# Holding the routing to one step behind each turned block, with the second expert's gathers issued in a row

## The chip, the cores and the metric

One core of one Trainium2 chip runs the whole program in one launch. The metric is the device time of one execution in microseconds (us); a kernel is timed in several runs and stands for the median. The engines are TensorE (PE, with its weight loads PEld), VectorE (DVE), ScalarE (ACT), GpSimd (POOL) and SyncE (SP, which issues most DMAs). Each works through its own queue in order and waits for the others by semaphores.

## The reference

Attention with a sigmoid in place of a softmax gives 3584 rows of 768 numbers. A greedy router gives each row to one of 8 experts, 448 rows each, and the expert applies two matrix products with a ReLU between.

```python
scores = scale * np.matmul(q, k.transpose(0, 1, 3, 2)) - np.log(S)      # 8 x 12 heads, S = 448, head_dim 64
attn = 1.0 / (1.0 + np.exp(-scores)); x = attn @ v                      # as [3584, 768]
logits = x @ w_gate                                                     # [3584, 8]
# all (token, expert) pairs from the highest logit down: a token takes an expert
# if the token is free and the expert has fewer than 448 tokens
for e in range(8):
    h = np.maximum(x[assigned == e] @ w1[e], 0.0)                       # [448, 768] @ [768, 1024]
    out[assigned == e] = h @ w2[e]                                      # [448, 1024] @ [1024, 768]
```

## The kernel before, in words

The first 300 us are attention; they are not touched. The router then fills one expert after another, in the order in which experts become full: phase 0 ahead of the first expert, phases 1 to 7 beside the experts' products.

An expert is 320 matmuls of the generator `moe` (356 for the first, which cuts its first tile in two): 144 for the first layer (lines 673, 675, 677: rows `xh`, `xl` against weights `wh`, `wl`, three products for one, since each fp32 number is split in a high and a low part), then 176 for the second layer (line 715) in two halves of four units of 22. A weight unit is loaded by SP three units ahead and split two units ahead: `wh` on ACT (line 598), `wl` on POOL (line 600).

Between two experts stands the next expert's input. `gather` (line 620, POOL) fetches four blocks of rows (128, 128, 128 and 64) into `xr` by the list `r_idx`. `xturn` (lines 634 to 638) turns a block in two halves: three PE transposes into a PSUM tile `tp`, of which there are two, then `xh` on ACT, then `xl` on DVE; `xl` is the last reader, so the next block's transposes wait for it. `scatter` (lines 645 and 646, POOL) writes an expert's result rows, four blocks again.

Routing phases are nearly all DVE work. A phase is a generator: `remove` (lines 302 to 306) and `keys` (lines 147 to 154, ending in `r_KT`), then two PE transposes of `r_KT` (line 163), the copy `r_KE` and 16 search steps (lines 174 to 213: three counts over 224 numbers, then small operations), then `pick`, `place` (line 253 to 264) and `lists` (lines 273 to 294), which leaves `r_idx`.

Nothing is scheduled by a tool. The loop at the end of `moe_attention` draws one matmul at a time from `moe(kx)` and adds its planned cost to a clock of its own (189 ns in the first layer, 164 ns in the second). By that clock it writes a routing step when the one before has had its planned time plus `SLACK` (every 2175 ns for a search step), and at most one item of the list `chores` (gathers, turns, scatters, each with a due time) every 1000 ns. What is still due when an expert ends is written at once by `flush`. So the clock sets only the order of the instructions; the times come from the engines.

Of the kernel before, what the change touches and what calls it, by code (L numbers as in the profile page):

```python
# [28 lines left out]
T_KEYS, T_KE, T_STEP, T_DVE, T_KAP, T_PICK, T_TOT, T_OH, T_BT = 3600, 2100, 2050, 2025, 500, 2600, 600, 3800, 600  # L29
SLACK = 150  # L30
CHORE_NS = 1000
TURN_NS = 2500
H_POOL = 8
EARLY = 1
FIRST = 4000.0
# [300 lines left out]
def moe_attention(tc, q, k, v, w_gate, w1, w2, out):  # L336
# [7 lines left out]
    with contextlib.ExitStack() as ctx:  # L344
# [269 lines left out]
        def blocks():  # L614
            for j in range(4):
                yield j, min(128, S - 128 * j)

        def gather(kx, j, n):
            t = xg[kx, j] = xp.tile([128, DM], F32, name="xr", bufs=XR_BUFS)
            nc.gpsimd.indirect_dma_start(out=t[:n], out_offset=None, in_=xs,  # L620
                                         in_offset=bass.IndirectOffsetOnAxis(ap=listed[kx][:n, j:j + 1], axis=0))

        def xturn(kx, j, n, hf, wide):
            if (j, hf) == (0, 0):
                XH[kx] = (xp.tile([128, ND, S], F32R, name="xh", bufs=2),
                          xp.tile([128, ND, S], F32R, name="xl", bufs=2))
            xh, xl = XH[kx]
            if wide and hf:
                p = ps_s.tile([128, 2, 512], F32, name="sc")[:, 0]
            else:  # L630
                p = ps_t.tile([128, 512], F32, name="tp")
            for i in range(3):
                dd = hf * 3 + i
                nc.tensor.transpose(p[:, i * n:(i + 1) * n], xg[kx, j][:n, dd * 128:(dd + 1) * 128], ident[:n, :n])  # L634
            pv = p[:, :3 * n].rearrange("p (a t) -> p a t", a=3)
            sl = (slice(None), slice(hf * 3, hf * 3 + 3), slice(j * 128, j * 128 + n))
            nc.scalar.activation(xh[sl], pv, AF.Copy)
            nc.vector.tensor_tensor(xl[sl], pv, xh[sl].bitcast(F32), OP.subtract)  # L638

        scat, chores = [], []  # L640
# [105 lines left out]
        for j, n in blocks():  # L746
# [5 lines left out]
            if j == 1:  # L752
                for _ in range(EARLY):
                    next(route)
        t_route, t_chore = FIRST, 1500.0
        for kx in range(E):
            turned = kx + 1 == E
            start = clock[0]

            def prepare():  # L760
                t0 = clock[0]
                lag = max(5000, min(14000, start + 40000 - t0))
                for j, n in blocks():
                    chores.append((t0 + 1500 * j, kx + 1, lambda j=j, n=n: gather(kx + 1, j, n)))
                for j, n in blocks():
                    chores.append((t0 + lag + TURN_NS * j, kx + 1,
                                   lambda j=j, n=n: [xturn(kx + 1, j, n, hf, False) for hf in range(2)]))

            def flush(kx):
                for c in [c for c in chores if c[1] <= kx]:  # L770
                    chores.remove(c)
                    c[2]()

            for step, cost in enumerate(moe(kx)):
                clock[0] += cost
                t = clock[0]
                if kx == 0 and step == 35:
                    flush(0)
                if t >= t_route:
                    t_route = t + next(route, 0) + SLACK  # L780
                if not turned and kx + 1 in listed:
                    prepare()
                    turned = True
                if t >= t_chore:
                    c = next((c for c in chores if c[0] <= t), None)
                    if c:
                        chores.remove(c)
                        c[2]()
                        t_chore = t + CHORE_NS
            if not turned:  # L790
                while kx + 1 not in listed:
                    next(route)
                prepare()
            flush(kx + 1)
# [28 lines left out]
```

## Time and profile before

| | |
|---|---|
| median of 3 runs | 876.28 us (876.18 to 877.7) |
| the profiled execution | 874.18 us, of which 872.4 us are the span of the profile |
| PE busy in the span | 823.4 us (94%), 5523 matmuls |
| DVE busy | 533.9 us (61%) |
| ACT, POOL busy | 437.9 us (50%), 485.5 us (56%) |
| first matmul of experts 0 to 7 | 328.8, 401.8, 469.6, 536.8, 605.3, 671.9, 739.3, 803.7 us |

A row of the timeline has the start in us from the span's start, the duration in us, the engine, the line, the operation with its output and inputs, and in brackets how long the engine had idled before it and who ended that. PE rows overlap: in the second layer a matmul's row is 0.33 to 0.34 us long and the next one starts 0.17 us after it. Experts are numbered from 0 in the order in which they run.

### The profile page before, as it was taken

The numbers are of one execution on the slowest core, as the hardware profiler recorded it, in microseconds if no ns is written. First come the engines' busy times: TensorE is split into PE (matmuls) and PEld (weight loads), VectorE is DVE, ScalarE is ACT, GpSimd is POOL, SyncE is SP. The second block draws the span as 40 slices with busy tenths as digits, with TensorE's granted clock in tenths as the row PEclk, the third lists the DMA queues.
The fourth block names the chain that finished last, engine by engine and source line by source line (L and its number), as shares of the span: only waits on it lengthen the run. The fifth ranks groups of instructions, "written<-read, shape, count | busy, mean of one in ns | idle before, by whom it ended". The sixth has DMA issues, their size and how long they took to land.

```text
span 872.4 us, 16402 instructions
## 1 busy us (share of the span) xinstructions
PE 823.4 (94%) x5523; PEld 650.5 (75%) x5523; DVE 533.9 (61%) x2047; ACT 437.9 (50%) x602; POOL 485.5 (56%) x510
## 2 busy tenths in 40 slices
PE   6999999999998829998999999999999999999996
PEld 3455455455455719998989889898899899899996
DVE  4665555555554978969879889789699620221211
ACT  6777777777775714424424433443434343444431
POOL 9645444444400024866865875865785874853643
PEclk9999999999999958999999999999999999999998
DMA  9876656666612954344354443452553543533421
GB/s 171 172 144 127 132 122 122 129 124 126 131 38 81 323 192 134 107 149 150 110 153 138 112 152 136 113 170 91 154 154 109 162 136 120 190 121 106 147 81 64
DMA packets 195573, 117.60 MB, mean 135 GB/s; under 512 B 144192, under 2 KB 185152, under 8 KB 195488
## 3 DMA queue, kind: packets, MB, share of 16 engines
q1 hardware_dynamic: 182752, 83.03, 36.6%
q0 software_dynamic: 10880, 33.28, 12.2%
q8 instruction: 44, 0.72, 0.4%
q10 hardware_dynamic: 1856, 0.23, 0.2%
q14 instruction: 41, 0.34, 0.1%
HBM read 94.47 MB, written 22.02 MB: 134 GB/s over the span
## 4 chain that ended last, share of the span: by engine, by line
PE 80%; DVE 11%; POOL 3%; issue 2%; DMA 2%; SPq 1%; ACT 0%; ACTq 0%; POOLq 0%; DVEq 0%
PE sc L715 22%; PE tp L463 13%; PE sc L439 11%; PE sc L675 8%; PE sc L673 8%; PE sc L677 8%; DVE r_junk L174 4%; PE tp L469 3%; PE sc L449 2%; PE tp L634 2%; PE tp L484 1%; POOL out_dram L646 1%; POOL xr L620 1%; PE rt L285 1%; POOL wl L600 1%
## 5 line engine op out<-in xcount | busy, mean ns | idle before, releaser
L600 POOL TENSOR_TENSOR wl<-wr,wh 128x768 fp32r<-128x768 f32 x110 | 202.3, 1853 | 32.3 <-ACT wh L598 32.0
L715 PE MATMUL sc<-wh,hb 128*128 128x384 f32 x768 | 200.4, 339 | 0.0
L429 ACT ACTIVATE at<-sc,bias 128x896 f32<-128x896 f32 x168 | 160.9, 1006 | 63.2 <-PE sc L449 38.2
L374 POOL DMA_DIRECT2D nkq<-in_q_dram x188 | 118.3, 645 | 111.6 <-DVE kqT L414 104.8
L677 PE MATMUL sc<-xh,wl 128*128 128x448 f32 (+2 forms) x396 | 144.6, 365 | 1.4 <-POOL wl L600 1.4
L675 PE MATMUL sc<-xl,wh 128*128 128x448 f32 (+2 forms) x396 | 144.9, 366 | 0.0
L673 PE MATMUL sc<-xh,wh 128*128 128x448 f32 (+2 forms) x396 | 144.9, 366 | 0.0
L715 PEld LDWEIGHTS sc<-wh,hb 128*128 128x128 f32 x768 | 138.1, 188 | 1.8 <-issue 0.7
L715 PE MATMUL sc<-wl,hb 128*128 128x384 f32 x384 | 129.5, 337 | 0.3 <-POOL wl L600 0.3
L598 ACT ACTIVATE wh<-wr 128x768 fp32r<-128x768 f32 x128 | 104.1, 851 | 51.0 <-PE sc L715 30.7
L174 DVE TENSOR_SCALAR_CACHE_REDUCE r_junk<-r_KE,r_T 128x224 bf16<-128x224 f32 x315 | 123.3, 441 | 0.1
L463 PE MATMUL tp<-at,nv 128*64 128x448 f32 x576 | 118.6, 547 | 0.0
L683 ACT ACTIVATE hb<-sc 128x768 fp32r<-128x768 f32 x32 | 26.0, 814 | 142.4 <-PE sc L677 142.4
L423 DVE TENSOR_TENSOR kqL<-kqT,kqH 128x896 fp32r<-128x896 f32 (+1 forms) x49 | 52.5, 1072 | 58.3 <-ACT kqH L421 58.2
L689 POOL TENSOR_TENSOR hb<-h,hb 128x768 fp32r<-128x768 f32 x32 | 59.2, 1850 | 49.9 <-ACT h L686 46.7
L620 POOL DMA_INDIRECT xr<-xs,r_idx x32 | 31.5, 984 | 96.5 <-ACT wh L598 79.8
L600 DVE TENSOR_TENSOR wl<-wr,wh 128x768 fp32r<-128x768 f32 x18 | 23.8, 1329 | 96.9 <-ACT wh L598 96.8
L463 PEld LDWEIGHTS tp<-at,nv 128*64 128x64 f32 x576 | 37.1, 136 | 59.4 <-issue 58.0
L677 PEld LDWEIGHTS sc<-xh,wl 128*128 128x128 f32 x396 | 75.0, 189 | 8.2 <-POOL wl L600 1.7
L675 PEld LDWEIGHTS sc<-xl,wh 128*128 128x128 f32 x396 | 75.1, 190 | 7.0 <-DVE xl L638 0.4
L673 PEld LDWEIGHTS sc<-xh,wh 128*128 128x128 f32 x396 | 75.1, 190 | 6.8 <-issue 0.4
L715 PEld LDWEIGHTS sc<-wl,hb 128*128 128x128 f32 x384 | 72.1, 188 | 0.8 <-POOL wl L600 0.6
(163 smaller groups left out, 1257.2 us busy)
## 6 DMA issues: line engine op xcount, KB each, us to landing
wr<-in_moe_w_dram SPq DMA_DIRECT2D x128, 384.0 KB, 3.2
xs<-xr SPq DMA_DIRECT2D x32, 336.0 KB, 4.3
nkq<-in_k_dram SPq DMA_DIRECT2D x190, 56.0 KB, 2.6
nkq<-in_q_dram POOLq DMA_DIRECT2D x188, 56.0 KB, 2.7
nv<-in_v_dram SPq DMA_DIRECT2D x92, 96.0 KB, 2.4
nr<-in_v_dram SPq DMA_DIRECT2D x46, 32.0 KB, 2.3
xr<-xs,r_idx POOLq DMA_INDIRECT x32, 4.6
out_dram<-yr,r_idx POOLq DMA_INDIRECT x32, 3.6
```

Source lines behind the costliest of these rows:

```text
L174: nc.vector.tensor_scalar(junk, KE, T[:, i:i + 1].bitcast(F32), None, OP.is_ge, OP.add, accum_out=cnt[:, i:i + 1])
L374: qn.dma_start(t[o:o + 32, n], rws[x])
L429: nc.scalar.activation(a, p[:, :, :S], AF.Sigmoid, bias=bias, scale=1 / math.sqrt(D))
L439: nc.tensor.matmul(p[:, j, :S], R[half, c * 128:(c + 1) * 128], M[half], start=i == 0, stop=i == 2)
L463: nc.tensor.matmul(p[j * 64:j * 64 + 64, :S], nat["v", b, g][:, h0 + j, c, :], AT[b, pr, c][:, j, :], start=(c == 0), stop=(c == 2 and pr ...
L598: nc.scalar.activation(hi, raw[u], AF.Copy)
L600: eng.tensor_tensor(lo, raw[u], hi.bitcast(F32), OP.subtract)
L673: nc.tensor.matmul(ph[:, f, lo:hi], wh[:, a, fs], xh[:, dd, lo:hi], start=st, stop=False)
L675: nc.tensor.matmul(ph[:, f, lo:hi], wh[:, a, fs], xl[:, dd, lo:hi], start=False, stop=False)
L677: nc.tensor.matmul(ph[:, f, lo:hi], wl[:, a, fs], xh[:, dd, lo:hi], start=False, stop=en)
L689: nc.gpsimd.tensor_tensor(h2, h0[:, :, t], h1.bitcast(F32), OP.subtract)
L715: nc.tensor.matmul(o, hs, w[:, a], start=st and n == 0, stop=en and n == len(terms) - 1)
```

## The change

When the next expert's list is done, `prepare` enters its gathers and turns in `chores`. Three things differ.

- While blocks remain to be turned, from 2500 ns (`HOLD_NS`) before the first is due, a routing step is written only if a block has been turned since the last one: one step behind each block at most. Ahead of the second expert (`kx` = 0) not even that: no routing step until all four blocks are turned.
- Blocks are due every 3200 ns of the planned clock in place of 2500; ahead of the second expert every 1300.
- The second expert's four gathers are written in a row, at once.

```diff
-TURN_NS = 2500
+TURN_NS = 3200
+TURN_FIRST = 1300
+HOLD_NS = 2500
...
             def prepare():
                 t0 = clock[0]
                 lag = max(5000, min(14000, start + 40000 - t0))
-                for j, n in blocks():
-                    chores.append((t0 + 1500 * j, kx + 1, lambda j=j, n=n: gather(kx + 1, j, n)))
-                for j, n in blocks():
-                    chores.append((t0 + lag + TURN_NS * j, kx + 1,
-                                   lambda j=j, n=n: [xturn(kx + 1, j, n, hf, False) for hf in range(2)]))
+                if kx:
+                    for j, n in blocks():
+                        chores.append((t0 + 1500 * j, kx + 1, lambda j=j, n=n: gather(kx + 1, j, n)))
+                else:
+                    for j, n in blocks():
+                        gather(1, j, n)
+
+                def turn_block(j, n):
+                    for hf in range(2):
+                        xturn(kx + 1, j, n, hf, False)
+                    turning["left"] -= 1
+                    turning["step"] = kx > 0
+
+                turning.update({"left": 4, "from": t0 + lag - HOLD_NS, "step": False})
+                for j, n in blocks():
+                    chores.append((t0 + lag + (TURN_NS if kx else TURN_FIRST) * j, kx + 1,
+                                   lambda j=j, n=n: turn_block(j, n)))
...
-                if t >= t_route:
+                if t >= t_route and (turning["left"] == 0 or t < turning["from"] or turning["step"]):
+                    turning["step"] = False
                     t_route = t + next(route, 0) + SLACK
```

Since the constants take two lines more, lines of the changed kernel carry a number that is 2 higher (638 becomes 640); the instructions are the same ones, and SP's queue is unchanged.

The held routing comes later as a whole. By the planned clock, counted in matmuls of the running expert, the third expert's list is done at matmul 252 of 320 in place of 221, the fourth's at 228 in place of 183, the fifth's at 213 in place of 143, the sixth's at 198 in place of 109, the seventh's at 184 in place of 75. Turns now stand at these matmuls: 328, 336, 344, 352 of 356 ahead of expert 1; 287, 302 and then two at the very end (320) ahead of expert 2; 263, 278, 298, 318 ahead of expert 3; 248, 263, 283, 303 ahead of expert 4; 233, 248, 268, 288 ahead of expert 5; 221, 241, 260, 280 ahead of expert 6; 75, 92, 108, 125 of expert 6 itself ahead of expert 7.

The order of DVE's queue where expert 1's blocks are turned, at the end of expert 0. Before, from the first search step's last operation (`r_T` is the step's result, `r_junk` and `c_CN` its counts, `r_ct`, `r_s`, `r_j` and `r_J` its small work) to the second block:

```order
L207 TENSOR_SCALAR r_T<-c_kk,r_J 128x3
L638 TENSOR_TENSOR xl<-tp,xh 128x3x128 x2
L174 TENSOR_SCALAR r_junk,c_CN<-r_KE,r_T 128x224 x3
L190 STREAM_TRANSPOSE r_ct<-c_CN 128x32
L192 TENSOR_SCALAR rt<-c_kk,r_J 128x3
L194 TENSOR_REDUCE r_s_5096<-r_ct 128x2
L196 STREAM_TRANSPOSE r_ct<-r_s_5096 128x32
L198 TENSOR_SCALAR r_j_5092,r_acc<-r_ct 128x3
L211 SCALAR_TENSOR_TENSOR r_T<-r_acc,rt 128x3
L213 TENSOR_SCALAR r_J<-r_acc,r_J 128x1
L638 TENSOR_TENSOR xl<-tp,xh 128x3x128 x2
```

The changed kernel at the same place, from the end of `keys`:

```order
L156 SCALAR_TENSOR_TENSOR r_KT<-rt,ML 112x256
L640 TENSOR_TENSOR xl<-tp,xh 128x3x128 x6
L640 TENSOR_TENSOR xl<-tp,xh 128x3x64 x2
L168 COPY r_KE<-rt 128x224
L176 TENSOR_SCALAR r_junk,c_CN<-r_KE,c_c_410 128x224 x3
L192 STREAM_TRANSPOSE r_ct<-c_CN 128x32
L196 TENSOR_REDUCE r_s_5127<-r_ct 128x2
```

All eight `xl` stand in a row now, and the phase's first search step behind them; before, a search step stood ahead of each of the first three blocks.

PE's queue at the end of expert 1, before the change, around the last block for expert 2 (the L634 row of 128x64), with the second layer going on behind it:

```order
L715 MATMUL sc<-wl,hb 128x384
L715 MATMUL sc<-wh,hr 128x384
L715 MATMUL sc<-wl,hr 128x384
L715 MATMUL sc<-wh,hb 128x384
L634 MATMUL tp<-ident,xr 128x64 x6
L715 MATMUL sc<-wh,hb 128x384
L715 MATMUL sc<-wl,hb 128x384
L715 MATMUL sc<-wh,hb 128x384 x2
```

The changed kernel at the end of expert 1:

```order
L717 MATMUL sc<-wh,hr 128x384
L717 MATMUL sc<-wl,hr 128x384
L636 MATMUL tp<-ident,xr 128x128 x6
L636 MATMUL tp<-ident,xr 128x64 x6
L675 MATMUL sc<-xh,wh 128x448
L677 MATMUL sc<-xl,wh 128x448
L679 MATMUL sc<-xh,wl 128x448
L675 MATMUL sc<-xh,wh 128x448
```

The last two blocks for expert 2 follow each other directly, behind the last matmul of expert 1 and ahead of the first of expert 2 (L675 here); before, all four stood between second-layer matmuls.

POOL's queue at the start of expert 1, before (`yr` is the result of expert 0, `out_dram` its scatters, `hb` and `hr` the first layer's output of expert 1):

```order
L645 MEMSET spacer 1x1
L646 DMA out_dram<-yr,r_idx 3584x768
L730 TENSOR_TENSOR yr<-yr,rest 64x384
L600 TENSOR_TENSOR wl<-wr,wh 128x768
L645 MEMSET spacer 1x1
L646 DMA out_dram<-yr,r_idx 3584x768
L645 MEMSET spacer 1x1
L646 DMA out_dram<-yr,r_idx 3584x768
L645 MEMSET spacer 1x1
L646 DMA out_dram<-yr,r_idx 3584x768
L600 TENSOR_TENSOR wl<-wr,wh 128x768
L689 TENSOR_TENSOR hb<-h_5308,hb 128x2x384
```

The changed kernel:

```order
L602 TENSOR_TENSOR wl<-wr,wh 128x768
L647 MEMSET spacer 1x1
L648 DMA out_dram<-yr,r_idx 3584x768
L647 MEMSET spacer 1x1
L648 DMA out_dram<-yr,r_idx 3584x768
L647 MEMSET spacer 1x1
L648 DMA out_dram<-yr,r_idx 3584x768
L602 TENSOR_TENSOR wl<-wr,wh 128x768
L647 MEMSET spacer 1x1
L648 DMA out_dram<-yr,r_idx 3584x768
L691 TENSOR_TENSOR hb<-h_5268,hb 128x2x384
L691 TENSOR_TENSOR hr<-h_5268,hr 128x2x64
```

All four scatters of expert 0 now stand behind the start of expert 1, the fourth between the second `wl` and the first `hb`; before, the first stood ahead of `yr`. The same is new at the start of expert 3; at the starts of experts 2, 4, 5 and 6 this piece stands as it did.

More of the change, by code (lines that the diff above doesn't have):

```diff
@@ L755, in moe_attention @@
         t_route, t_chore = FIRST, 1500.0
+        turning = {"left": 0, "from": 0.0, "step": False}
         for kx in range(E):
```

## The prediction

> **What bounds the kernel now.** I read the page's head first, then the waits of PE from 300 us on, then PE's timeline around each of them.
>
> ```profile
> PE 823.4 (94%) x5523; PEld 650.5 (75%) x5523; DVE 533.9 (61%) x2047; ACT 437.9 (50%) x602; POOL 485.5 (56%) x510
> ```
>
> PE is the bound, and the change neither adds nor takes a PE instruction. So what it can win is PE's idle time while the experts run, and what it can lose is new idle time. The waits of PE from 300 us on (total, times, longest; only rows of the experts' stage are copied, since the rows left out belong to phase 0 or the first input, ahead of anything that moves):
>
> ```profile
> PE tp L634 <- DVE xl L638: 6.2, 4, 2.2
> ...
> PE rt L163 <- DVE r_KT L154: 1.7, 5, 0.4
> PE sc L677 <- POOL wl L600: 1.4, 1, 1.4
> ...
> PE sc L715 <- POOL wl L600: 0.3, 1, 0.3
> ```
>
> Four times PE waits for `xl` with a turn, five times for the end of `keys`, twice for POOL: 9.6 us in all. PE's timeline shows what the gap column leaves out:
>
> ```profile
> 390.10 0.38 PE L163 MATMUL rt<-ident,r_KT 112*128 112x112 f32 x2 [0.39 <-DVE r_KT L154]
> ...
> 392.26 0.82 PE L634 MATMUL tp<-ident,xr 128*128 128x128 f32 x6
> 392.84 0.42 PE L715 MATMUL sc<-wl,hr 128*128 128x384 f32 x1
> ...
> 397.28 0.33 PE L715 MATMUL sc<-wh,hr 128*128 128x384 f32 x1
> 397.45 0.34 PE L715 MATMUL sc<-wl,hr 128*128 128x384 f32 x1
> 397.70 1.01 PE L634 MATMUL tp<-ident,xr 128*128 128x128 f32 x6
> 400.95 0.86 PE L634 MATMUL tp<-ident,xr 64*128 64x64 f32 x6 [2.24 <-DVE xl L638]
> 401.77 0.47 PE L673 MATMUL sc<-xh,wh 128*128 128x448 f32 x1
> ...
> 458.30 1.01 PE L634 MATMUL tp<-ident,xr 128*128 128x128 f32 x6 [1.42 <-DVE xl L638]
> ...
> 465.32 0.58 PE L634 MATMUL tp<-ident,xr 64*128 64x64 f32 x6
> 465.83 0.44 PE L715 MATMUL sc<-wh,hb 128*128 128x384 f32 x1
> ...
> 520.30 1.01 PE L634 MATMUL tp<-ident,xr 128*128 128x128 f32 x6 [0.59 <-DVE xl L638]
> ...
> 592.10 1.01 PE L634 MATMUL tp<-ident,xr 128*128 128x128 f32 x6 [1.94 <-DVE xl L638]
> ...
> 646.43 0.44 PE L715 MATMUL sc<-wl,hb 128*128 128x384 f32 x1 [0.31 <-POOL wl L600]
> ```
>
> A gap is counted from the end of the row before, and that end lies 0.17 us behind the time at which the next matmul could have started (397.28 is followed by 397.45). So each gap costs about 0.17 more than it says. An undisturbed block takes 0.58 us of PE (392.26 to 392.84), the short one 0.51 (465.32 to 465.83).
>
> Why `xl` is late: DVE works in order, and a routing step stands between the blocks.
>
> ```profile
> 458.64 0.43 DVE L174 TENSOR_SCALAR_CACHE_REDUCE r_junk<-r_KE,r_T 128x224 bf16<-128x224 f32 x1
> ...
> 460.95 1.01 DVE L638 TENSOR_TENSOR xl<-tp,xh 128x384 fp32r<-128x384 f32 x2
> 461.88 0.44 DVE L174 TENSOR_SCALAR_CACHE_REDUCE r_junk<-r_KE,r_T 128x224 bf16<-128x224 f32 x1
> ```
>
> A step takes 2.31 us (458.64 to 460.95), the two `xl` of a block 0.93, so DVE needs 3.24 us for a block and a step. Blocks were due every 2500 ns of the planned clock, 15 matmuls of 0.17 plus the block itself: some 3.2 us of PE. DVE has no spare time, and whatever makes it late once stays.
>
> **What the change takes away.** Durations are from the profiled execution, 874.18 us.
>
> Expert 0 to 1: with no step among the blocks, the wait for the last block goes. From 397.70 to 400.95 are 3.25 us where 0.58 would do, and from 400.95 to 401.77 are 0.82 where 0.51 would: 2.98. The cover is sound: a block every 8 matmuls and 0.58 is some 2.0 us, and a block's `xl` pair ends about 1.95 us after its first transpose when DVE is free (0.5 to `xh`, 0.43 for one `xh`, two `xl`), the first of the pair 0.5 earlier, which is the buffer that is needed first.
>
> Experts 1 to 2, 2 to 3, 3 to 4: gaps 1.42, 0.59, 1.94 plus three times 0.17, 4.46. In the new order blocks are 15 and then 20 matmuls apart (3.2 and 4.1 us) with one step behind each, so DVE's 3.24 us fit, with 0.8 us over at the wider ones. What is late next is the end of expert 1; it is priced below.
>
> The five waits for `keys`: the transposes of `r_KT` stood 3750 ns of the planned clock behind `keys`, which was 0.3 to 0.4 us too early. They now stand behind the first block, 5740 ns behind `keys` (in expert 0 behind the last, 9000). All 1.7 us go, and 5 times 0.17: 2.55.
>
> The POOL wait at 646.43 came with gathers among the first layer's POOL work; in expert 4 they move to the second layer, where no `hb` competes. 0.31 and 0.17: 0.48.
>
> Together 10.5 us.
>
> **What it adds.**
>
> The end of expert 1. Its last two blocks are written together behind the last matmul, as the last two of expert 0 were before. That place is the price list, with its ACT and DVE rows:
>
> ```profile
> 397.82 0.48 ACT L723 COPY yr<-sc 128x384 f32<-128x384 f32 x1 [0.88 <-PE sc L715]
> ...
> 399.18 0.86 ACT L637 ACTIVATE xh<-tp 128x384 fp32r<-128x384 f32 x2
> ...
> 400.35 1.01 DVE L638 TENSOR_TENSOR xl<-tp,xh 128x384 fp32r<-128x384 f32 x2
> ```
>
> ACT must first copy the expert's result (three copies from 397.82), so `xh` starts 1.48 us after the block's first transpose, and `xl` could have started at 399.61 (399.18 and 0.43); it started at 400.35 because of a step. Of the 2.98 us, 0.74 were the step, and 2.24 remain with DVE free. I add 2.24. From below: nothing, if ACT were early; from above 2.98 plus what the next rows show.
>
> That row is the first search step's last operation, 0.23 us at its best:
>
> ```profile
> 393.71 0.23 DVE L207 TENSOR_SCALAR r_T<-c_kk,r_J 128x3 int32<-128x3 int32 x1
> ...
> 455.57 2.22 DVE L207 TENSOR_SCALAR r_T<-c_kk,r_J 128x3 int32<-128x3 int32 x1
> 455.92 1.84 POOL L600 TENSOR_TENSOR wl<-wr,wh 128x768 fp32r<-128x768 f32 x1
> ...
> 577.10 1.80 DVE L207 TENSOR_SCALAR r_T<-c_kk,r_J 128x3 int32<-128x3 int32 x1
> ```
>
> Twice it took 2 us, ending with POOL's `wl` (455.92 and 1.84 is 457.76, 455.57 and 2.22 is 457.79). It now stands between the first block and the second of experts 2 to 5. There the wider spacing of the later blocks takes it up, but ahead of expert 2 only some 0.8 us are spare before the two blocks at the end. I add 0.4, between 0 and 1.2 (2.22 less 0.23 and 0.8).
>
> [...]
>
> The last block ahead of expert 3 stands two matmuls from the end, where the next expert's first products need its `xh` and `xl`. Before, with none between, that cost 0.31 (0.82 against 0.51). I take 0.25, between 0 and 0.5.
>
> POOL at the starts of experts 1 and 3. A fourth scatter now stands ahead of the first `hb`. Expert 3 before, and the place where POOL was late, in expert 6:
>
> ```profile
> 536.80 0.36 PE L673 MATMUL sc<-xh,wh 128*128 128x448 f32 x1
> ...
> 543.81 0.09 POOL L645 MEMSET spacer<- 1x1 f32 x1
> ...
> 545.05 1.85 POOL L600 TENSOR_TENSOR wl<-wr,wh 128x768 fp32r<-128x768 f32 x1
> 546.85 1.84 POOL L689 TENSOR_TENSOR hb<-h,hb 128x768 fp32r<-128x768 f32 x1
> ...
> 549.07 1.83 POOL L600 TENSOR_TENSOR wl<-wr,wh 128x768 fp32r<-128x768 f32 x1
> ...
> 739.30 0.36 PE L673 MATMUL sc<-xh,wh 128*128 128x448 f32 x1
> ...
> 754.17 0.37 PE L673 MATMUL sc<-xh,wh 128*128 128x448 f32 x1
> 754.38 0.37 PE L675 MATMUL sc<-xl,wh 128*128 128x448 f32 x1
> 756.09 0.47 PE L677 MATMUL sc<-xh,wl 128*128 128x448 f32 x1 [1.35 <-POOL wl L600]
> ```
>
> In expert 6 the matmul that needs the `wl` of the fifth unit could have started at 754.58 (754.17 and 754.38 are 0.2 apart), 15.3 us after the expert's first. In expert 3 that `wl` is the one at 549.07; it ends at 550.9, 14.1 us after the first. A scatter with its memset costs POOL 1.24 us (543.81 to 545.05), and the result's last add comes up to 0.3 later. That makes 15.3 to 15.6, so a wait of 0 to 0.3 plus 0.17 at each of the two starts. I add 0.6 together, between 0 and 3.0 (twice the 1.35 and 0.17 of expert 6).
>
> Expert 5: `place` and `lists` of the last phase now stand among the turns. DVE needs at most 4.4 us from the one product to the next, since those 25 matmuls before covered it without a wait. Now an `xl` pair stands ahead, which ends 1.95 us after its block's start: 6.35 us, and the product comes 26 matmuls, two blocks and 0.4 us of small products after that start, 6.1. I add 0.2, between 0 and 1.
>
> The four gathers in a row: POOL's next `wl` comes two gathers later, some 2.5 us by the scatter's 1.24, but feeds a unit 44 matmuls on, 7.6 us. Their landing stays ahead of the turns:
>
> ```profile
> 385.82 0.97 POOL L620 DMA_INDIRECT xr<-xs,r_idx  x1 [1.28 <-DVE rt L302]
> ...
> DMA to landing us min/median/max: 3.8/4.6/5.4
> ```
>
> The first block is now turned at about 391.0 (392.26 less four matmuls and the `keys` stall), 5.2 us after the issue. That costs nothing at the median, 0.2 at the maximum. SP's queue does not change, and the later lists only move the gathers; they are all issued 6 us ahead of their turn as before.
>
> **The sum.** 10.5 taken away; 2.24, 0.4, 0.25, 0.6 and 0.2 added, 3.7. The net is 6.8 us off 874.18, thus 867.4 for that execution. The runs' median, 876.28, lies 2.1 above it, and the same difference gives **869.5 us**.
>
> **The rivals.**
>
> *Half of it stays.* The steps may not be the cause of the later waits: two of the three (1.42 at 458.30, 1.94 at 592.10) follow a slow L207, and L207 still stands between the blocks. Then only expert 0 to 1 (2.98), `keys` (2.55) and POOL (0.48) are won, 6.0, against 3.3 added (all but the 0.4): 2.7 net, 873.6 us. For it: the rows above. Against it: the wider spacing gives DVE 0.8 us at two blocks of each later expert, and PE waits only when two buffers are both full.
>
> *POOL takes over, and the kernel is slower.* If the `wl` of the fifth unit were late in each of experts 1 to 5 as in expert 6, 5 times 1.52 is 7.6 in place of the 0.6 counted, a net of +0.2 and 876.5 us; from 1.5 us each on it is slower, and at 2 each it would be 878.9. For it: expert 6 shows the mechanism, and experts 2, 4 and 5 have little over. Against it: at their starts POOL's order is as before, when none of them waited, and they lose their gathers from the first layer.
>
> *The additions are hidden.* If ACT's copies run early enough at the end of expert 1 and POOL holds, 3 of the 3.7 us go: 866.5 us.
>
> **How the numbers follow.** The forecast 0.64, with a range of its own of 867.8 to 871.5; half of it 0.17; additions hidden 0.10; POOL 0.04; something that no row shows, of no or bad effect, 0.05. The range for 8 in 10 reaches from 866.8 to 873.6: it leaves out the slower cases and half of the hidden one. A measurement tells about 0.2%, 1.75 us. Faster than 874.5: the first three, nearly, 0.88. Slower than 878.0: 0.05, from POOL and the unnamed. The same: 0.07.
>
> **What would show it.** In the changed profile the waits of PE for `keys` are gone; the wait for `xl` has one row left, 1.4 to 2.5 us at the end of expert 1, and the first expert's end shows eight `xl` without a step; expert 1 starts near 398.5 in place of 401.77; the waits for POOL are 1.35 in expert 6 and under 0.5 in experts 1 and 3. The forecast is wrong if `xl` waits stand at other turns (half of it), if POOL's total is over 4 us, or if a turn waits for its gather.

## The result, and the profile after

The changed kernel takes 869.26 us (median of 5 runs, 868.01 to 871.66), where the kernel before takes 876.28 (875.99 to 877.7, 5 runs): a ratio (time after over time before) of 0.9923, 95% interval 0.9908 to 0.9939. Run again in a later series it took 869.90 (6 runs, 869.41 to 870.22) against 875.41, a ratio of 0.9932 (0.9919 to 0.9945). The forecast was 869.5, with 866.8 to 873.6 for 8 in 10.

The profiled execution is the longest of its five, 871.66 us with a span of 869.8, so the two traces differ by only 2.5 us where the medians differ by 7.0. What the trace places is therefore less than what the runs show, and part of the reading below goes by the trace of the second series, whose execution (869.41) lies near its median.

The busy times of the page's head, changed kernel:

```profile
PE 824.0 (95%) x5523; PEld 652.3 (75%) x5523; DVE 537.3 (62%) x2047; ACT 437.9 (50%) x602; POOL 485.6 (56%) x510
```

PE has the same instructions and 0.6 us more busy time. The waits of PE from 300 us on (total, times, longest; rows of phase 0 and of the first input left out):

```profile
PE tp L636 <- DVE xl L640: 2.7, 3, 1.9
...
PE sc L679 <- POOL wl L602: 1.6, 2, 1.4
...
PE tp L636 <- DVE r_ct L198: 0.7, 1, 0.7
PE sc L677 <- DVE xl L640: 0.6, 1, 0.6
```

The five waits at L165 for `keys` are gone, and of 6.2 us behind `xl` 2.7 remain at turns. But there are three of those, not one, and two rows are new: a turn that names `r_ct`, and the first `xl` product of expert 3. The timeline shows the places (start, duration, engine, line, instruction, and in brackets the idle time before it):

```profile
397.85 0.58 PE L636 MATMUL tp<-ident,xr 64*128 64x64 f32 x6
...
399.20 0.37 PE L675 MATMUL sc<-xh,wh 128*128 128x448 f32 x1
...
460.98 0.85 PE L636 MATMUL tp<-ident,xr 128*128 128x128 f32 x6 [0.69 <-DVE r_ct L198]
...
464.64 0.82 PE L636 MATMUL tp<-ident,xr 128*128 128x128 f32 x6
...
464.84 0.48 ACT L725 COPY yr<-sc 128x384 f32<-128x384 f32 x1 [0.93 <-PE sc L717]
...
466.19 0.86 ACT L639 ACTIVATE xh<-tp 128x384 fp32r<-128x384 f32 x2
...
467.32 0.86 PE L636 MATMUL tp<-ident,xr 64*128 64x64 f32 x6 [1.86 <-DVE xl L640]
...
468.14 0.47 PE L675 MATMUL sc<-xh,wh 128*128 128x448 f32 x1
468.53 0.69 PE L677 MATMUL sc<-xl,wh 128*128 128x448 f32 x1
...
469.39 0.57 PE L675 MATMUL sc<-xh,wh 128*128 128x448 f32 x1
469.76 0.57 PE L677 MATMUL sc<-xl,wh 128*128 128x448 f32 x1
...
526.88 3.65 POOL L602 TENSOR_TENSOR wl<-wr,wh 128x768 fp32r<-128x768 f32 x2
...
527.42 0.21 DVE L207 TENSOR_SCALAR r_J<-r_PF,r_J 128x1 int32<-128x1 int32 x1
...
527.67 2.89 DVE L209 TENSOR_SCALAR r_T<-c_kk,r_J 128x3 int32<-128x3 int32 x1
...
530.48 1.01 DVE L640 TENSOR_TENSOR xl<-tp,xh 128x384 fp32r<-128x384 f32 x2
...
531.07 1.01 PE L636 MATMUL tp<-ident,xr 128*128 128x128 f32 x6 [0.59 <-DVE xl L640]
...
537.38 0.47 PE L677 MATMUL sc<-xl,wh 128*128 128x448 f32 x1 [0.60 <-DVE xl L640]
```

In the trace of the second series the rows behind `xl` are two (1.86 at the end of expert 1, 0.28 ahead of expert 5), and one of its turns waits for a gather:

```profile
525.28 0.85 PE L636 MATMUL tp<-ident,xr 128*128 128x128 f32 x6 [0.41 <-DMA xr<-xs,r_idx]
...
526.41 1.09 DVE L209 TENSOR_SCALAR r_T<-c_kk,r_J 128x3 int32<-128x3 int32 x1
```

Four readings. The end of expert 0 is clean, and expert 1 starts at 399.20 in place of 401.77. The end of expert 1 carries the priced pair of blocks: from 464.64 to 468.14 are 3.50 us for 1.09 of work (0.58 and 0.51), 2.41 lost. Behind that gap the matmuls are 0.37 us apart in place of 0.20, for about 3.4 us: the granted clock, the share of its full speed at which TensorE was let run, is 0.59 from 469.24 to 472.64 (0.50 from 468.40 to 471.80 in the second trace). And ahead of expert 3 the search step's last operation, L209, took 2.89 us; its end, 530.56, is that of POOL's second `wl` (526.88 and 3.65 is 530.53), and the turn behind it waits. The first `xl` product of expert 3 (537.38) waits too. In the second trace L209 took 1.09 us at this place, ending with the first of the two `wl` (525.61 and 1.85 is 527.46), and neither of the two waits is there.

The turn at 460.98 names an operation of DVE that had long ended. Its gather is the late one; the view of the tile `xr` from 450 to 463 us has its four gathers:

```profile
DMA to landing us min/median/max: 3.5/6.5/7.1
```

The gather that this turn reads was issued at 454.05, 6.9 us before.

What each expert lasts, from its first matmul to the next expert's first, out of the timelines (us; the forecast is the prediction's terms put where they fall, a `keys` wait as 0.5):

| expert | before | forecast of the change | changed, first trace | changed, second trace | second less before |
|---|---|---|---|---|---|
| 0 | 73.01 | -3.5 | 69.93 | 70.06 | -2.95 |
| 1 | 67.82 | +0.8 | 68.94 | 68.04 | +0.22 |
| 2 | 67.21 | -1.0 | 68.17 | 67.65 | +0.44 |
| 3 | 68.53 | -2.3 | 66.19 | 65.81 | -2.72 |
| 4 | 66.53 | -1.0 | 66.33 | 66.33 | -0.20 |
| 5 | 67.45 | +0.2 | 67.79 | 67.79 | +0.34 |
| 6 | 64.39 | 0 | 64.42 | 64.42 | +0.03 |

The forecast's -6.8 stands against -4.8. Experts 1 and 3 did better, 0, 2 and 4 worse.

### The profile page after: what moved, and what is told of

It is laid out like the page before. It is cut to its first block, busy times and chain, and to the rows that moved or that the text cites. A ratio compares the mean times of both kernels' runs of the same rounds, so it can differ in the third digit from the quotient of the medians.

```text
span 869.8 us, 16399 instructions
## 1 busy us (share of the span) xinstructions
PE 824.0 (95%) x5523; PEld 652.3 (75%) x5523; DVE 537.3 (62%) x2047; ACT 437.9 (50%) x602; POOL 485.6 (56%) x510
## 4 chain that ended last, share of the span: by engine, by line
PE 83%; DVE 7%; POOL 4%; issue 2%; DMA 1%; ACT 1%; SPq 1%; POOLq 0%; DVEq 0%; ACTq 0%
PE sc L717 26%; PE tp L465 13%; PE sc L441 11%; PE sc L679 8%; PE sc L677 8%; PE sc L675 8%; DVE r_junk L176 3%; PE tp L471 3%; PE sc L451 2%; PE tp L636 1%; POOL out_dram L648 1%; PE tp L486 1%; POOL wl L602 1%; PE rt L287 1%; DVE xl L640 1%
## 5 line engine op out<-in xcount | busy, mean ns | idle before, releaser
L675 PE MATMUL sc<-xh,wh 128*128 128x448 f32 (+2 forms) x396 | 145.0, 366 | 0.0
L675 PEld LDWEIGHTS sc<-xh,wh 128*128 128x128 f32 x396 | 75.4, 190 | 6.7
L602 DVE TENSOR_TENSOR wl<-wr,wh 128x768 fp32r<-128x768 f32 x18 | 25.9, 1441 | 81.0 <-ACT wh L600 80.9
```

Source lines behind the costliest of these rows:

```text
L602: eng.tensor_tensor(lo, raw[u], hi.bitcast(F32), OP.subtract)
L675: nc.tensor.matmul(ph[:, f, lo:hi], wh[:, a, fs], xh[:, dd, lo:hi], start=st, stop=False)
```

## The experiments

Twelve runs in four series, each beside runs of the kernel before on the same chip. The theory is that of the prediction: the routing steps among the turns were the lost time, and the hold takes them out; what is left over lies in L209, in the pair at the end of expert 1 and in the half-speed stretch behind it. Rivals are that the spacing alone does it, that the gain lies in the first expert alone, or that it lies in the clock.

**The changed kernel again**, to see how much of 871.66 belongs to that execution.

> The changed kernel once more, as the measure for the three kernels beside it. Theory A (what is left is the pair of blocks at the end of expert 1, and PE's clock falling to half behind it in some executions): the median is within 1.5 us of 869.3, and over the runs the time falls as the granted clock rises: about 871.5 at a clock of 0.981, 868 to 869.5 at 0.983 to 0.985. Theory B (the spread between runs has nothing to do with PE's clock): slow and fast runs have the same clock.

869.90 us, ratio 0.9932 (0.9919 to 0.9945). The gain repeats. Its six runs lie within 0.8 us at granted clocks of 0.982 and 0.983, so the spread of 3.6 us that the first five had (clocks 0.981 to 0.985) did not come back, and whether time falls as the clock rises can't be read from them.

**The constant of the first search step in PSUM.** L209 reads `K.kk[:, 1]` from SBUF; here a copy is made in PSUM ahead of the search.

```diff
+        if not pe:
+            nc.vector.tensor_scalar(X[:, 8:11], K.kk[:, 1], 0, None, OP.bitwise_xor)
         for st in range(16):
...
-                nc.vector.tensor_scalar(T, K.kk[:, 1], nJ, None, OP.bitwise_xor)
+                nc.vector.tensor_scalar(T, K.kk[:, 1] if pe else X[:, 8:11], nJ, None, OP.bitwise_xor)
```

> The changed kernel, with the constant that the first search step's last operation reads copied to PSUM ahead of the search (one more small VectorE operation in each of phases 1 to 6). Theory A (that operation waits for GpSimd's tensor operations because both of its tensor operands lie in SBUF): each of its instances takes 0.3 us or less, the waits for xl in experts 2 and 4 are gone, and the time is 0.5 to 1.5 us below the changed kernel. Theory B (the operation is slow for another reason, or its delay never reaches PE outside expert 1's end): instances of 1.8 us and more remain, or they are gone and the time is within 0.4 us.

867.33 us (4 runs, 866.86 to 867.72), ratio 0.9902 (0.9884 to 0.9919): 2.6 below the changed kernel of the same series, more than expected. The line's own rows from 380 us on (number, then shortest, median and longest in ns), changed kernel, first trace:

```profile
L209 DVE TENSOR_SCALAR r_T<-c_kk,r_J x5: 228/981/2890, 402.4 to 656.9; 128x3 int32<-128x3 int32 x5
```

and with the source in PSUM, where the line is 211:

```profile
L211 DVE TENSOR_SCALAR r_T<-rt,r_J x5: 220/221/224, 401.2 to 653.3; 128x3 int32<-128x3 int32 x5
```

All five now take 0.22 us. Ahead of expert 3, where POOL's two `wl` run from 524.59 for 3.66 us in this trace, the `xl` behind it starts at 525.55. That is the cause shown: with source and result in SBUF, this operation took 0.66 to 2.89 us at the four places of the first trace where a `wl` was running, and with its source in PSUM it did not wait. The changed kernel's own trace has a sister to it, L194, which reads the same constant in SBUF and writes to PSUM:

```profile
L194 DVE TENSOR_SCALAR rt<-c_kk,r_J x70: 180/182/185, 405.2 to 691.8; 128x3 int32<-128x3 int32 x70
```

It never took longer than 0.185 us, though 27 of the 70 ran from start to end beside a running `wl`. Not every operation with both in SBUF waits, either: L207 just ahead of it, 128x1 and with both in SBUF too, took 0.21 us during the same `wl` (527.42, above). In the traces of this series expert 4, where a turn had waited 0.28 behind L209, became 0.65 us shorter. Experts 1 and 2 became 0.19 and 0.40 shorter, but no wait behind L209 stood there: in expert 2 it is the turn at 525.28 that no longer waits for its gather. Another 0.65 lies in expert 0, which was granted a clock of 0.82 in place of 0.68 between 328 and 334 us, and the edit does not explain that. So the medians of this series differ by 2.6 us, of which these two traces place at most 0.65 on the operation; a cleaner price of it comes with the last version but one, below.

The wait can be longer than one POOL instruction: 2.89 us here, and 3.97 below, where a gather's issue lasts 0.91 and one `wl` 1.81 to 1.86. At three other places of the first trace (402.37, 592.40 and 656.90) the operation ended within 0.04 us of the end of the `wl` that was running when it began, as in the second trace (527.50 against 527.46). At the fifth, 461.81, POOL ran nothing beside it, and it took 0.23.

**The hold of the second expert for all of them**: no step at all until the four blocks are turned, gathers in a row, blocks every 1300 ns, everywhere.

```diff
-                if kx:
-                    for j, n in blocks():
-                        chores.append((t0 + 1500 * j, kx + 1, lambda j=j, n=n: gather(kx + 1, j, n)))
-                else:
-                    for j, n in blocks():
-                        gather(1, j, n)
+                for j, n in blocks():
+                    gather(kx + 1, j, n)
...
-                    turning["step"] = kx > 0
+                    turning["step"] = False
...
-                    chores.append((t0 + lag + (TURN_NS if kx else TURN_FIRST) * j, kx + 1,
+                    chores.append((t0 + lag + TURN_FIRST * j, kx + 1,
```

> Every expert gets what the change gives the second one: four gathers in a row, blocks 1300 ns apart, no routing step among them. The planned order then ends all turns 2 us or more ahead of the expert's end. Theory A (the changed kernel still loses at the end of expert 1, 2.2 us and half a clock for 3.4 us behind it in some runs, and at the first search step between blocks): 3 to 4 us below the changed kernel, about 865.8, no wait for xl left, clock 0.985 in all runs. Theory B (a step behind each block is hidden, and the later routing or the gathers in a row cost elsewhere): within 1 us of the changed kernel or slower, with new waits for POOL or for the gathers.

869.15 us (6 runs, 867.81 to 872.93), ratio 0.9926 (0.9905 to 0.9946): no better than the changed kernel. The 3 to 4 us of theory A did not come; theory B did, and the timeline of expert 3's end says why:

```profile
579.97 1.01 POOL L732 TENSOR_TENSOR yr<-yr,rest 64x384 f32<-64x384 f32 x1 [7.65 <-ACT yr L731]
580.95 1.84 POOL L602 TENSOR_TENSOR wl<-wr,wh 128x768 fp32r<-128x768 f32 x1
582.94 0.99 POOL L622 DMA_INDIRECT xr<-xs,r_idx  x1 [0.16 <-DVE rt L153]
...
587.62 1.54 PE L636 MATMUL tp<-ident,xr 128*128 128x128 f32 x6 [2.81 <-DMA xr<-xs,r_idx]
```

Written in a row, the first gather stood behind an addition on POOL that waits 7.65 us for ACT and behind a `wl`. It went out too late for a turn that the hold had made early: 2.81 us, and half speed behind it (a granted clock of 0.59 from 587.00 to 590.40). Expert 3 lasted 70.39 us in place of 65.81, while experts 1 and 2 were 2.1 and 1.5 shorter (65.96 and 66.19). In expert 6 the gathers among the `wl` cost a wait of 2.56 where 1.35 had been.

**The full hold with the constant in PSUM.**

> The hold for every expert and the constant in PSUM together. Theory A: with no search step among the blocks the slow operation no longer matters, so this is within 0.5 us of the hold for every expert alone. Theory B (the slow operation costs wherever it stands): 0.5 us or more below it.

870.52 us (6 runs, 869.09 to 872.74), ratio 0.9935 (0.9921 to 0.9949). The late gather decides here too (2.87 us). The version without the copy has no wait behind `xl` among PE's waits (its rows are 3.0 us behind gathers and 2.8 behind `wl`), so there was nothing to give back, and theory B's 0.5 us or more did not come. Why it is 1.4 us slower is not settled; the ranges overlap.

**Only the first part** (the second expert's hold, gathers and spacing; the others as before).

```diff
-                turning.update({"left": 4, "from": t0 + lag - HOLD_NS, "step": False})
+                turning.update({"left": 0 if kx else 4, "from": t0 + lag - HOLD_NS, "step": False})
...
-                    chores.append((t0 + lag + (TURN_NS if kx else TURN_FIRST) * j, kx + 1,
+                    chores.append((t0 + lag + (2500 if kx else TURN_FIRST) * j, kx + 1,
...
-                if t >= t_route and (turning["left"] == 0 or t < turning["from"] or turning["step"]):
+                if t >= t_route and (turning["left"] <= 0 or t < turning["from"] or turning["step"]):
```

The last line, with `<= 0`, belongs to the next two versions too: a count that starts at 0 falls below it with each block and must not bring the hold back.

> The change's treatment of the second expert alone (gathers in a row, 1300 ns, no step among the blocks); all later experts as before the change, 2500 ns and no hold. By the planned order the third expert's list comes 5 us later than before, and its blocks stand nearer to the end of expert 1, with routing steps between. Theory A (the steps among the blocks are the cost): expert 0 ends 3.4 us earlier than before (2.98 and 0.5 for the keys), the later waits for xl and keys remain, 1 to 2 us are added at the end of expert 1; 1 to 3 us below before, 873 to 875. Theory C (the second expert is where nearly all of the gain lies): 5 us or more below before.

871.27 us (6 runs, 870.74 to 872.59), ratio 0.9939 (0.9921 to 0.9958), lower than expected. Expert 0 became 4.07 us shorter (68.94) where 3.4 was said; from 329.89 us on its first matmuls, of 128x256, start 0.12 us apart in this trace, and 0.21 apart from 329.62 to 331.75 in that of the kernel before, where the granted clock is 0.74 from 328.80 to 334.80. But expert 3 too lost 2.26 us (66.27), although steps stood among its turns: the routing came later as a whole, and the waits of 0.59 and 1.94 are gone. What is left behind `xl` stands at the end of expert 1, 0.94 at the last turn and 1.75 at expert 2's first `xl` product (467.71 is the start of that `xl`, right behind a search step):

```profile
468.12 0.47 PE L677 MATMUL sc<-xl,wh 128*128 128x448 f32 x1 [1.75 <-DVE xl L640]
```

That the later waits come from steps among turns is thus not shown by this run for experts 2 and 3; they also depend on which step stands there.

**Only the later experts** (the second expert as before).

```diff
-                if kx:
-                    for j, n in blocks():
-                        chores.append((t0 + 1500 * j, kx + 1, lambda j=j, n=n: gather(kx + 1, j, n)))
-                else:
-                    for j, n in blocks():
-                        gather(1, j, n)
+                for j, n in blocks():
+                    chores.append((t0 + 1500 * j, kx + 1, lambda j=j, n=n: gather(kx + 1, j, n)))
...
-                turning.update({"left": 4, "from": t0 + lag - HOLD_NS, "step": False})
+                turning.update({"left": 4 if kx else 0, "from": t0 + lag - HOLD_NS, "step": False})
...
-                    chores.append((t0 + lag + (TURN_NS if kx else TURN_FIRST) * j, kx + 1,
+                    chores.append((t0 + lag + (TURN_NS if kx else 2500) * j, kx + 1,
```

> The change for the later experts alone (3200 ns, one step behind each block); the second expert's input as before. The third expert's list is then as early as before and no blocks pile up at the end of expert 1. Theory A: the waits for xl at experts 2 to 4 (4.5 us), four of five waits for keys (2.0) and the POOL wait (0.5) go, the first search step gives back about 1; 5 to 6.5 us below before, about 870.5, thus nearly all of the whole change's gain, since the whole change pays for its first part at the end of expert 1. Theory C: 2 us or less below before.

870.38 us (6 runs, 869.50 to 870.83), ratio 0.9923 (0.9906 to 0.9941): as much as the whole change. PE's waits:

```profile
PE tp L636 <- DVE xl L640: 2.9, 2, 2.2
```

The 2.24 at the end of expert 0 is there as before (expert 0 lasts 73.25). But expert 1 lasts 67.06, 1.0 to 1.9 less than in the changed kernel, because its list is done earlier and no pair of blocks falls behind its last matmul. The two parts gave 0.61% and 0.77% apart and 0.7 to 0.8% together: what the hold wins at the end of expert 0, it gives back in large part at the end of expert 1.

**Spacing alone for the later experts** (3200 ns, without the hold).

```diff
-                turning.update({"left": 4, "from": t0 + lag - HOLD_NS, "step": False})
+                turning.update({"left": 0 if kx else 4, "from": t0 + lag - HOLD_NS, "step": False})
```

> The changed kernel without the hold for the later experts: blocks 3200 ns apart, but routing steps written whenever they are due, so that 1 or 2 stand between blocks. Theory A (one step behind each block at most is what counts): VectorE needs 2.3 us for each step and 0.9 for a block, so where two steps fall between blocks PE waits again; the five waits for keys return but one; 1.5 to 4 us above the changed kernel. Theory D (the wider spacing alone does it): within 0.7 us of the changed kernel.

872.93 us (7 runs, 871.69 to 873.83), ratio 0.9953 (0.9936 to 0.9971).

```profile
PE tp L636 <- DVE xl L640: 3.7, 2, 3.3
```

One wait of 3.3 us stands at the end of expert 1, where steps come between the blocks again. The hold is worth some 1.8 to 2.6 us beside the spacing (0.0021 and 0.0030 of 877, by the changed kernel's ratios of 0.9932 and 0.9923; the changed kernel was not in this series, and the intervals overlap). The rival, that the spacing does it, falls within the series: with 2500 ns and no hold for the later experts it was 871.27, and the wider spacing alone is no faster (872.93; the ranges overlap).

**The full hold, with the turns 3 us further behind the list.** If the late gather was the fault of the full hold, a larger lag mends it. Expert 6 keeps its gathers one by one.

```diff
-                lag = max(5000, min(14000, start + 40000 - t0))
+                lag = max(8000 if kx > 1 else 5000, min(14000, start + 40000 - t0))
...
-                if kx:
+                if kx == 6:
...
+                    else:
+                        gather(kx + 1, j, n)
...
-                    turning["step"] = kx > 0
+                    turning["step"] = False
...
-                    chores.append((t0 + lag + (TURN_NS if kx else TURN_FIRST) * j, kx + 1,
+                    chores.append((t0 + lag + TURN_FIRST * j, kx + 1,
```

> The hold for every expert, with its two losses mended: from the third expert on the first block is due 8000 ns behind the list in place of 5000, so that a gather queued behind GpSimd's other work lands in time, and the last expert's gathers are spread as in the changed kernel. Theory A (the hold for every expert lost at experts 3 and 6 what it won at 1, 2 and 4): expert 3 falls from 70.4 to about 66 us, expert 6 from 65.6 to 64.4, no wait for xl or for a gather stays beyond 0.5 us, PE's clock never falls to half between 330 and 870 us, and the time is 864 to 866 in every run. Theory B (holding all steps delays the routing, which costs elsewhere): 868 or more.

867.34 us (5 runs, 866.68 to 867.49), ratio 0.9894 (0.9876 to 0.9911): better than the changed kernel by the ratios (0.9932 and 0.9923, from other series), and short of the 864 to 866 expected. No turn waits for a gather and no pair stands at the end of expert 1 (65.99 us). What is left, of PE's waits:

```profile
PE sc L679 <- POOL wl L602: 1.6, 2, 1.4
PE tp L636 <- DVE xl L640: 1.3, 1, 1.3
PE rt L165 <- DVE r_KT L156: 1.1, 3, 0.4
```

The hold begins 2500 ns ahead of the first turn, which now stands further behind the list, so the `keys` come before it again. And L209 in expert 4 is the worst of all:

```profile
652.25 0.91 POOL L622 DMA_INDIRECT xr<-xs,r_idx  x1 [0.30 <-issue]
...
652.86 3.97 DVE L209 TENSOR_SCALAR r_T<-c_kk,r_J 128x3 int32<-128x3 int32 x1
653.17 3.62 POOL L602 TENSOR_TENSOR wl<-wr,wh 128x768 fp32r<-128x768 f32 x2
...
657.35 1.01 PE L636 MATMUL tp<-ident,xr 128*128 128x128 f32 x6 [1.26 <-DVE xl L640]
```

It started while a gather was being issued and ended with the second `wl` behind it (656.79). Expert 4 lasts 67.92 us here, 1.6 more than in the changed kernel.

**Expert 6's gathers later**, at 12 us behind the list and 3.6 us apart by the planned clock, out of the way of the first `wl`.

```diff
-                lag = max(8000 if kx > 1 else 5000, min(14000, start + 40000 - t0))
+                lag = 36000 if kx == 6 else max(8000 if kx > 1 else 5000, min(14000, start + 40000 - t0))
...
-                        chores.append((t0 + 1500 * j, kx + 1, lambda j=j, n=n: gather(kx + 1, j, n)))
+                        chores.append((t0 + 12000 + 3600 * j, kx + 1, lambda j=j, n=n: gather(kx + 1, j, n)))
```

> As the one above, and the last expert's gathers start 12000 ns into expert 6, 3600 ns apart, behind the first wl's, with its blocks turned from 36000 ns on. Theory A (the wait of 1.35 us for POOL in expert 6 comes from scatters and gathers ahead of the fifth unit's wl): that wait goes, expert 6 takes 62.8 to 63.0 us in place of 64.4, 1.5 us below the one above. Theory B (POOL is late there for its other work): the wait stays, and the time is the same within 0.4 us.

865.90 us (5 runs, 865.70 to 866.42), ratio 0.9880 (0.9863 to 0.9897): 1.44 less, for a wait of 1.35 and its 0.17. Expert 6 lasts 63.11 us in place of 64.39.

**The constant in PSUM again**, beside these two.

> The changed kernel with the constant in PSUM once more, beside the two above: 867.3 within 1 us, that is 2 us above the first of them by theory A.

867.25 us (6 runs, 866.21 to 868.77), ratio 0.9896 (0.9879 to 0.9913): the ratio of 0.9902 is there again on a second chip. (The expectation's 2 us above the larger lag did not come, because that version had missed its own forecast.) This pair of traces of one kernel also gives the price of the half-speed stretch, since the order and the gap are the same (1.86 and 1.87 us at the end of expert 1) and only one has it. Columns: window, its length, busy times of PE, PEld, DVE, ACT, POOL, then the granted clock, the DMA share and GB/s. First series:

```profile
467.00:470.40 3.40, 3.40 (x12) 3.07 (x11) 3.23 (x23) 0.74 (x2) 2.94 (x4) 0.54 0.11 26
470.40:473.80 3.40, 3.40 (x18) 3.15 (x17) 3.16 (x22) 0.00 (x0) 3.16 (x4) 1.00 0.99 364
```

and second:

```profile
467.40:470.80 3.40, 3.40 (x19) 3.15 (x18) 3.23 (x22) 0.85 (x2) 2.97 (x4) 1.00 0.08 13
```

12 matmuls in 3.4 us against 19: expert 2 lasts 67.25 us with it and 65.65 without, 1.60.

**Both together**: the hold with the larger lag, late gathers in expert 6, and the constant in PSUM.

> The kernel with the hold behind the lists and expert 6's late gathers, 865.9 us, and beside it the constant that the first search step's last operation (L209) reads is copied to PSUM ahead of the search. Theory A (that operation waits through GpSimd's operations only as long as its source lies in SBUF, as the shorter runs with the source in PSUM suggest): the wait of 1.26 us for xl in expert 4, behind L209's 3.97 us, goes, and with the smaller ones some 1.3 to 1.6 us: 864.4 us, from 864.0 to 865.0. Rival (the operation waits for something else, or the gain of the constant in PSUM seen before came from the clock alone): 865.9 us, L209 as long as before.

864.74 us (4 runs, 864.54 to 864.99), ratio 0.9862 (0.9839 to 0.9886): 1.16 below the version without the copy, which ran on another chip (0.0018 by the ratios, 1.6 us), a little short of 864.4 and within the bounds. At the place of the 3.97 us:

```profile
653.51 0.22 DVE L211 TENSOR_SCALAR r_T<-rt,r_J 128x3 int32<-128x3 int32 x1
653.81 3.63 POOL L604 TENSOR_TENSOR wl<-wr,wh 128x768 fp32r<-128x768 f32 x2
...
655.55 1.02 DVE L642 TENSOR_TENSOR xl<-tp,xh 128x384 fp32r<-128x384 f32 x2 [1.81 <-ACT xh L641]
```

DVE now idles ahead of `xl`, and no turn waits for it. Expert 4 lasts 66.31 us in place of 67.93, 1.62 less, where the wait was 1.26 and its 0.17, and the copy is the only edit between the two. In experts 2 and 3, where L209 had taken 1.13 and 1.99 us and no turn waited for it, the durations stay within 0.06 us: here the operation cost time only where a turn stood behind it.

**The transposes of `r_KT` later by 800 ns.**

```diff
-T_KEYS, T_KE, T_STEP, T_DVE, T_KAP, T_PICK, T_TOT, T_OH, T_BT = 3600, 2100, 2050, 2025, 500, 2600, 600, 3800, 600
+T_KEYS, T_KE, T_STEP, T_DVE, T_KAP, T_PICK, T_TOT, T_OH, T_BT = 4400, 2100, 2050, 2025, 500, 2600, 600, 3800, 600
```

> As the one before it, and beside it each list's transposes of r_KT are set later by 800 ns of the planned clock, so that VectorE's writing of keys comes ahead of them; the turns of rows stand where they stood. Theory A (a wait at L165 for keys is time that TensorE loses): the three waits, 1.1 us by their rows and 0.17 more for each, go, some 1.6 us: 862.9 us, from 862.4 to 863.8. Rival (the search is late by as much, and the wait goes to the turn or the gather behind it): as the one before it, 864.4 us, with a wait for xr or xl in place of that for keys.

863.75 us (4 runs, 863.34 to 865.43), ratio 0.9856 (0.9829 to 0.9882), the fastest of all; at 1.0 us below the one before it the step is within the expectation's bounds, though the two ranges overlap. PE's waits between 380 and 800 us are down to

```profile
PE tp L638 <- DMA xr<-xs,r_idx: 0.4, 1, 0.4
PE sc L681 <- POOL wl L604: 0.3, 1, 0.3
```

The three waits for `keys` are gone. Experts 2 and 3 became 0.57 and 0.58 us shorter, which is what their rows say (0.38 and 0.39, and 0.17 each). The rival holds for the third: in expert 4 a turn now waits 0.45 for its gather, and the expert is 0.21 longer. This version takes 1.4% less than the kernel before, and some 0.7% less than the changed kernel (0.9856 over 0.9923; they were not run in one series).

## Why the prediction was right, point by point

The time and the sign were right, the mechanism was right in the main, and the sum was better than its terms: it had some 2 us of cost too little against the traces, and an addition of 2.1 us that has nothing to do with the change covered it. Two of the three signs by which the prediction would call its forecast wrong did come: waits behind `xl` stood at turns other than the one at the end of expert 1 (0.59 and 0.28 in the first trace, 0.28 in the second), and in each trace one turn waited for its gather.

- **Expert 0 to 1** was said to give 2.98 and `keys` 0.56. The end is clean, the start of expert 1 came 2.57 us earlier than before in the first trace (399.20; 398.5 was said), and expert 0 lost 2.95 to 3.08. The missing 0.5 isn't separated from the clock granted between 328 and 334 us, which varied from 0.66 to 0.90 between traces of kernels that don't differ there.
- **The waits for `keys`** are gone, as said. That they cost PE what their rows say was tested at the end: two of three gave their 0.57 and 0.58, the third went to a gather, and the medians differ by 1.0 us where 1.6 was expected.
- **The end of expert 1** was priced at 2.24 and cost 2.41, which refutes the rival that the additions are hidden. The prediction left out what comes behind it: a clock of half speed for 3.4 us, 1.6 us by the pair of traces, in expert 2.
- **L209 is the step that failed.** "I add 0.4, between 0 and 1.2" for expert 2, and "the wider spacing of the later blocks takes it up". In expert 1, where the 0.4 was put, it took 0.23 us. In expert 2 it took 2.89 in the first trace and cost PE 0.59 and 0.17 at the turn, in the second 1.09 and cost nothing; in expert 4 it took 0.98 and cost 0.28 and 0.17 in both. The bound came from one POOL operation (1.84 us); here the operation waited through two (2.89), and in a later run through a gather's issue and two (3.97).
- **A gather that lands late.** Ahead of expert 2, 0.69 and 0.17 in the first trace and nothing in the second; ahead of expert 3, nothing in the first and 0.41 and 0.17 in the second. The prediction had 6 us between issue and turn against a landing of at most 5.4; here the longest was 7.1.
- **The last block ahead of expert 3** was put at 0.25, between 0 and 0.5. PE waited 0.60 and 0.17 in the first trace, since a step stood ahead of the block's `xl`; in the second, with the shorter L209 and the same order, it did not wait.
- **POOL** cost 0.29 and 0.17 in expert 1, nothing in expert 3 and 1.36 in expert 6, within the 0.6 said for the first two; the wait of 0.31 at 646.43 is gone, as said. The rival that POOL takes over is refuted.
- **The rival that half of it stays** is partly true: waits behind `xl` did remain at turns that follow L209, and L209 is why. Its 873.6 lies 4 us above what was measured, since the wait of 1.94 ahead of expert 4 went, and expert 3 lost 2.34 to 2.72 us.
- **The 2.1 us carried over** from the trace to the median were luck. The changed kernel's two traced executions lie 2.4 above and 0.5 below their medians, so the sum against the trace, 867.4, was 2.0 to 4.3 too low, and the addition covered it. Why most runs of the kernel before lie above its traced one is not settled; their granted clocks differ, from 0.978 with 879.5 and 879.8 us to 0.986 with 874.0.

## What to carry to other kernels

When two engines take turns on one path, take the third party out of the queue between them, but look at what the delayed work pushes to the next boundary: here the end of expert 0 was won and a good part given back at the end of expert 1. Before holding back work, check that the transfers behind it still go out early enough, by the longest landing and by what stands ahead of them on the queue that issues them. A small operation whose duration varies tenfold (0.23 to 2.22 us in the kernel before) is worth one look at what ran beside it: moving its source from SBUF to PSUM cost one copy of 0.15 us in each search, and the median then lay 2.6 us lower in one order of the queues and 1.2 in another.

## What the runs showed of the hardware

- A 128x3 int32 operation of VectorE with source and result in SBUF took 0.23 us at its best and up to 3.97 us beside GpSimd; at its longest it waited through a gather's issue and two `wl` in a row, and with the same order of the queues it once took 2.89, to the end of the second `wl`, and once 1.09, to the end of the first. With its source in PSUM it took 0.22 at all five places, and a like operation with its result in PSUM 0.18 at all 70. Why it once ended with the second `wl` and once with the first, and why its 128x1 neighbour didn't wait, was not tried.
- Behind gaps of PE of 1.75 to 3.32 us the clock was granted at about half for some 3.4 us, in some executions and not in others: 0.59 and 0.50 in the two traces of the changed kernel (1.86), 0.59 with the full hold (2.81), 0.51 with the spacing alone (3.32), 0.60 with only the first part (1.75, behind one of 0.94). With the same gap of 1.86 and 1.87 us, one trace has it (0.54) and one has not (1.00). Behind the gap of 2.24 us at the end of expert 0 the kernel before has 1.00 from 401.70 to 405.10, while in the run with only the later experts changed the matmuls lie 0.37 us apart from 403.05 to 406.40, in place of 0.20. What decides between the two cases stays open: an experiment that only shifts a gap in time was not made.
- The four gathers ahead of expert 2 (three of 128 rows, one of 64) landed between 3.5 and 7.1 us after their issue in the first trace of the changed kernel.
